# Three token blocks side by side in the second MLP product of the first batch, and weight pieces converted at other times

## The chip, the cores and the metric

The kernel runs on one core of a Trainium2 chip. The metric is the device time of one execution in microseconds (us); lower is better. A core has five engines that run their own instruction streams and wait for one another through semaphores: TensorE (PE: matrix products into the eight banks of PSUM, the accumulation memory), VectorE (DVE: elementwise work), ScalarE (ACT: activations and copies), GpSimd (POOL: elementwise work on SBUF, the on-chip memory) and SyncE (SP), which in this kernel issues every transfer from and to the main memory (HBM).

## The reference

For four batches of 768 tokens, eight heads of 40 features go through a gated recurrent cell; then a Fourier mixing and an MLP follow on rows of 320.

```python
# cell, for every time step
C = f_stab * C + i_stab * outer(v, k);  n = f_stab * n + i_stab * k
y = sigmoid(o_gate) * (C @ q) / max(|n . q|, 1)
# mixing and MLP, x = y with the heads side by side
mixed = real(fft(fft(x, axis=1), axis=2))
u = x + mixed
un = (u - mean(u)) / sqrt(var(u) + 1e-6)
out = u + relu(un @ w_ch1) @ w_ch2          # 320 -> 1280 -> 320
```

The two weight matrices reach the device as 64-bit floats, and the kernel turns them into 32-bit floats itself.

## The kernel before, in words

**The cell.** The recurrence is computed in chunks of 128 tokens (in two halves of 64 from the second batch on). For a chunk there are scores (`ps`), weights `W` that are loaded and passed through an exponential on ScalarE (L491), masked on GpSimd (L515) and multiplied with the scores on VectorE ("weighing", L672), the heads (`ph`), and the state `C`, to which VectorE adds each half's part (L667). The heads of a chunk are computed in two passes; between them ScalarE makes a copy of one element (L699) for which the second pass waits. VectorE finishes a chunk in five instructions (L712 to L720).

**The mixing.** VectorE folds the six blocks of 128 tokens in three steps (L812 to L824), TensorE multiplies by the sequence table (`pz`, `pzt`) and then by the feature table (`pu`), VectorE adds the result to x and takes mean and variance (L955 to L963), ScalarE centres the rows (`uc`, L971), TensorE transposes them (`put`, L978), and ScalarE copies that out (`uT`, L983).

**The MLP.** The six token blocks stand in two groups of three, in the order 0, 5, 1 and 4, 2, 3. For the first batch the first product (L1047, L1056) makes the hidden rows, one slot for each of ten blocks of 128 hidden units (f from 0 to 9) and each group; ScalarE applies the ReLU (L1071). The second product (`mlp_out`, L1181) accumulates over f in a bank `po`. It is cut into halves, f 0 to 4 and f 5 to 9, one slot each. When a block's product is complete, VectorE scales it and adds it to u (`residual`, L1187) and SP stores the block. The later batches use another scheme (L1118, L1237).

**The weights.** The 64-bit words are converted in ten pieces of 128x640: pieces 0 to 4 are the first weights, 5 to 9 the second, where piece 5 holds f 0 and 1, piece 6 f 2 and 3, and so on to piece 9 with f 8 and 9. A piece is loaded by SP into one of two buffers (`raw`, 640 KB), then *taken* by VectorE (L406, L408, which split exponent and mantissa bits into `e` and `m`, each with one buffer), *converted* by ScalarE (L413, L414) and *joined* by VectorE (L420, L422, L426). One piece must be joined before the next is taken. Pieces 3 and 4 are needed by the first product from the slots 35 and 36 on.

**What sets the order.** The program writes its order by hand. `at(slot, phase, fn)` enters a step in a plan, and `run` issues the plan sorted by slot and phase, so that each engine's instructions stand in that order. Within a slot the phases are EVAC 0, FILL 1, MAIN 2 and FILL_PE 3, with fractions between. The first batch's MLP begins in slot 31: slots 31 to 50 are the first product, slots 51 to 62 the second. The cell of the second batch runs beside it from slot 32, that of the third from slot 53, and the mixing of the second batch from slot 54. The list `when` gives slot and phase of each piece's take, convert and join; a piece after the fifth is loaded in the slot after the join of the piece two before. The pieces' own steps are in the class `Piece`:

```python
at(when[n - 2][2][0] + 1, FILL + 0.7, p.load)
for (s, phase), fn in zip(w, (p.take, p.convert, p.join)):
    at(s, FILL + phase, fn)
```

**The banks.** Four PSUM banks are handed out in the order of the string `turn`, a digit for each request of `bank`. From slot 28 on the scores and the heads of the cell have the other four.

**After the product.** `weight_sums` (L1096, four steps) forms sums of the first weights for the later batches, and `out_weight_sums` (L1209) sums of the second weights.

Of the kernel before, what the change touches and what calls it, by code (L numbers as in the profile page):

```python
# [19 lines left out]
L = 128  # L20
# [6 lines left out]
DM = H * D  # L27
DFF = 4 * DM
NFF = DFF // L
TAIL = DM - 2 * L  # L30
TG = NT // 2
# [22 lines left out]
def kernel(  # L54
# [14 lines left out]
    nc = tc.nc  # L69
# [13 lines left out]
    ps_early = ExitStack()  # L83
    ps_s, ps_h = (ps_early.enter_context(tc.tile_pool(name=n, bufs=2, space=PSUM)) for n in ("ps_s", "ps_h"))

    turn = iter("3210321032120312031230123012012301023130201320132013201320123021320321")

    def bank(name, shape, n=None):

        return ps_m.tile(shape, FP, name=name, tag=f"pm{next(turn) if n is None else n}")  # L90
# [16 lines left out]
    w2_sb = const.tile([L, NFF, DM], FP, name="w2_sb")  # L107
# [16 lines left out]
    def at(slot, phase, fn, *args):  # L124
        plan.setdefault((slot, phase), []).append((fn, args))
# [7 lines left out]
    EVAC, FILL, MAIN, FILL_PE = range(4)  # L133
# [248 lines left out]
    class Piece:  # L382
        def __init__(self, dst, src):
            self.dst, self.src, self.float = dst, src, src.dtype == FP
# [407 lines left out]

    class Mix:
        def __init__(self):
            self.pu, self.uc, self.pt, self.h = {}, {}, {}, {}

    mixes = {}

# [268 lines left out]
    def hidden(gr, f):  # L1067
        return hid[gr, f % 2][:, f // 2 * TG * L:(f // 2 + 1) * TG * L]
# [107 lines left out]
    def mlp_out(b, gr, i, half):  # L1176
        k = mixes[b]
        if half == 0:
            k.po = bank("po", [L, DM])
        for f in range(half * NFF // 2, (half + 1) * NFF // 2):  # L1180
            nc.tensor.matmul(k.po, hidden(gr, f)[:, i * L:(i + 1) * L], w2_sb[:, f, :], start=(f == 0), stop=(f == NFF - 1))  # L1181

    def residual(b, c, cols, po):

        k = mixes[b]
        u = k.u[:, c, cols]
        nc.vector.scalar_tensor_tensor(out=u, in0=po, scalar=k.rstd[:, c:c + 1], in1=u, op0=OP.mult, op1=OP.add)  # L1187

    def store(b, c):
        nc.sync.dma_start(out=out[b, c * L:(c + 1) * L, :], in_=xs[b][:, c, 0:DM])  # L1190

    def mlp_store(b, gr, i):
        c = ORDER[gr * TG + i]
        residual(b, c, slice(0, DM), mixes[b].po)
        store(b, c)


# [70 lines left out]
    def plan_mlp(b, s):  # L1268
        groups = range(NT // TG)
        for i in range(NFF // 2) if b > 0 else ():  # L1270
            for step in range(4):
                at(s, MAIN, mlp_block, b, i, step)
                s += 1
            end = i == NFF // 2 - 1
            for n, (gr, f) in enumerate(((1, 2 * i + 1), (1, 2 * i), (0, 2 * i))):
                at(*((s - 1, MAIN + (-0.1 if gr else 0.1)) if end else (s + n, MAIN + 0.5)), mlp_relu_in_place, gr, f)
        for gr in groups if b == 0 else ():
            for f in range(NFF):
                at(s, MAIN, mlp_in, b, gr, f)
                s += 1  # L1280
                if f % 2:
                    at(s, EVAC, mlp_relu, b, gr, f - 1)
                    at(s, EVAC, mlp_relu, b, gr, f)
        if b > 0:
            for j in range(1, 5):
                at(s - (5, 4, 3, 3)[j - 1], FILL_PE + 0.3, hidden_sums, 0, (j,), 0, NFF // 2 - 2)
            at(s, EVAC, hidden_sums, 0, (1, 2), NFF // 2 - 2, NFF // 2)
            at(s, MAIN + 0.1, hidden_sums, 0, (3, 4), NFF // 2 - 2, NFF // 2)
        for n in range(TG) if b > 0 else ():
            for step in range(4):  # L1290
                at(s, MAIN, mlp_out_pair, b, n, step)
                if n < TG - 1 and step > 1:
                    for j in (2 * step - 3, 2 * step - 2):
                        at(s, MAIN + 0.6, hidden_sums, n + 1, (j,))
                s += 1
        for gr in groups if b == 0 else ():
            for i in range(TG):
                for half in range(2):
                    at(s, MAIN, mlp_out, b, gr, i, half)
                    s += 1  # L1300
                at(s, EVAC, mlp_store, b, gr, i)

    ctx.enter_context(tc.manual_schedule())
    gates_pool = ExitStack()
# [3 lines left out]
    def plan_batch(b, s_mlstm, s_mix, s_mlp):  # L1308
        (plan_halves if b > 0 else plan_mlstm)(b, s_mlstm)
        done = [s_mlstm + n for n in ((16, 19, 22) if b == 0 else (18, 21, 22))]  # L1310
        assert s_mix >= done[-1] and s_mlp >= s_mix + 9
        late = [s_mlp + 2 * c for c in range(TG)]
        if b == 0:
            feat = [s_mix + 1, s_mix + 1, s_mlp + 3]
            turn = [s_mix + 2, s_mix + 3, s_mix + 4]
            add = turn + [s_mlp, s_mlp + 4, s_mlp + 5]
            late = [s_mlp + 2, s_mlp + 5, s_mlp + 7]
        else:
            feat = [s_mix + c for c in ((3, 4, 6) if b == 1 else (3, 4, 7))]
            add = [s_mix + c for c in ((4, 4, 5, 6, 7, 7) if b == 1 else (4, 5, 5, 6, 8, 9))]  # L1320
            turn = [s_mix + c for c in ((5, 6, 6) if b == 1 else (6, 7, 8))]
            late = [s_mix + c for c in ((7, 8, 8) if b == 1 else (9, 10, 10))]
            at(s_mlp, EVAC + 0.5, mlp_sums)
        plan_mix(b, s_mix, done, feat, add, turn + late)
        s = s_mlp + NFF + 2
        at(s, FILL + 0.6, mix_rstd, b)
        for n in range(3):
            at(s + 3 * n if b == 0 else s, FILL + 0.65, mix_rstd_step, b)
        plan_mlp(b, s_mlp)

    s_mlp = 31
# [2 lines left out]
    plan_batch(2, 53, 83, s_mlp + 2 * MLP_SLOTS)  # L1334
    plan_batch(3, 83, 115, s_mlp + 3 * MLP_SLOTS)
    for n in range(4):
        at(s_mlp + 2 * NFF + 1 + n, FILL + 0.4, weight_sums, n)
        at((56, 57, 58, 75)[n], FILL + 0.4, out_weight_sums, n)

    at(60, FILL + 0.4, lambda: nc.gpsimd.memset(ds_sb[0:1, 0, 0, :], 1.0))  # L1340

    when = [((2, 0.7), (4, 0.5), (6, 0.6)), ((6, 0.7), (7, 0.5), (8, 0.6)), ((11, 0.7), (13, 0.5), (22, 0.6))]
    when += [((22, 0.7), (23, 0.7), (27, 0.6)), ((27, 0.7), (28, 0.7), (32, 0.6))]
    when += [((33, 0.7), (34, 0.3), (34, 0.6)), ((34, 0.7), (35, 2.7), (36, 0.6))]
    when += [((s, 0.7), (s + 1, 0.7), (s + 2, 0.6)) for s in (36, 39, 42)]
    pieces = w1_pieces + w2_pieces
    for n, (w, p) in enumerate(zip(when, pieces)):
        if n > 4:
# [138 lines left out]
```

## Time and profile before

| | us |
|---|---|
| median of 3 runs | 402.24 (402.18 to 402.57) |
| the profiled execution | 402.53 |
| its span, first to last instruction | 400.8 |
| PE busy | 382.8 (96%) |
| DVE busy | 279.8 (70%) |
| ACT busy | 171.7 (43%) |
| POOL busy | 132.6 (33%) |
| L1181, the first batch's second product, 120 records | 34.2 busy, mean 0.435 |

Times are counted from the first instruction of the profiled execution. The profile shows two records of TensorE for each product that the program writes in 32-bit floats, so the 60 products of L1181 are 120 records. Matrix products overlap: a record lasts longer than the distance to the next. A line of the time-ordered view has the start, the duration, engine, line of the program, operation, output and inputs, the count, and in brackets the idle time of the engine before it and what released it. PEclk is the share of full speed at which TensorE's clock was granted.

### The profile page before, as it was taken

What the parts mean: (1) busy time and instruction counts of PE and PEld (TensorE: products, weight loads), DVE (VectorE), ACT (ScalarE), POOL (GpSimd) and SP (SyncE); (2) the same over time, 40 slices, a digit from 0 to 9 for tenths busy, and PEclk for the clock granted to TensorE, in tenths of its full rate; (3) what the DMA queues carried; (4) which work ended last, traced back from release to release, by engine and by line L of the source; (5) the groups of instructions that cost most, each with busy time, mean ns of one, the idle gap of its engine ahead of it and who ended that gap; (6) DMA issues with size and microseconds to landing.
All of it is one profiled execution on the core that took longest, in us unless ns stands there. A gap on an engine that the chain in (4) does not pass through costs nothing.

```text
span 400.8 us, 10588 instructions
## 1 busy us (share of the span) xinstructions
PE 382.8 (96%) x4174; PEld 278.4 (69%) x4174; DVE 279.8 (70%) x671; ACT 171.7 (43%) x481; POOL 132.6 (33%) x237
## 2 busy tenths in 40 slices
PE   8999899979999999998999989989999999999996
PEld 6877555545567677755569888845578986556996
DVE  7789988999665467485775598777764686336652
ACT  6987367655640232655462214544440023454000
POOL 5648513555863341253255124451310000020000
PEclk9999999979999999999999999999999999999999
DMA  7878499677286254447800526410000000000100
GB/s 222 288 228 246 151 241 275 191 191 220 72 190 169 60 155 127 118 133 185 186 1 28 138 71 194 145 38 2 0 0 18 17 34 33 2 0 0 34 33 34
DMA packets 25631, 44.78 MB, mean 112 GB/s; under 512 B 5727, under 2 KB 14766, under 8 KB 25454
## 3 DMA queue, kind: packets, MB, share of 16 engines
q1 hardware_dynamic: 25582, 44.11, 39.1%
q8 instruction: 33, 0.54, 0.6%
q14 instruction: 16, 0.13, 0.1%
HBM read 38.49 MB, written 4.12 MB: 106 GB/s over the span
## 4 chain that ended last, share of the span: by engine, by line
PE 67%; DVE 18%; DMA 6%; issue 4%; ACT 2%; POOL 1%; SPq 1%; DVEq 0%; POOLq 0%; ACTq 0%
PE po L1237 18%; PE pm L1118 14%; PE po L1181 8%; PE pm L1056 5%; PE ph L519 4%; PE pm L1123 4%; PE pu L935 3%; PE ps L519 2%; DMA Gb<-G_d 2%; DVE so L716 2%; DMA raw<-in_w 1%; PE pz L904 1%; PE pz L892 1%; DMA W<-M_d 1%; PE put L978 1%
## 5 line engine op out<-in xcount | busy, mean ns | idle before, releaser
L1187 DVE SCALAR_TENSOR_TENSOR x<-po,rstd,x 128x160 f32<-128x160 f32 (+1 forms) x69 | 27.0, 395 | 43.9 <-PE po L1237 36.8
L1127 DVE TENSOR_TENSOR h<-h,pm 128x384 f32<-128x384 f32 x60 | 30.5, 550 | 29.2 <-PE pm L1123 13.9
L652 POOL TENSOR_TENSOR C<-C,decB 128x164 f32<-128x164 f32 x30 | 16.0, 532 | 75.7 <-DVE C L667 64.7
L1118 PE MATMUL pm<-uT,w_sb 128*128 128x384 f32 x90 | 37.7, 506 | 2.1 <-DVE h L1127 1.3
L491 ACT ACTIVATE W<-W,colT 128x64 f32<-128x64 f32 x144 | 37.4, 339 | 0.0
L1181 PE MATMUL po<-w_sb,h 128*128 128x320 f32 x120 | 34.2, 435 | 0.0
L1056 PE MATMUL pm<-uT,w_sb 128*128 128x384 f32 x80 | 31.2, 528 | 0.3 <-DVE x L955 0.2
L515 POOL TENSOR_SCALAR_AFFINE_SELECT W<-W 64x512 f32<-64x512 f32 x36 | 27.2, 756 | 11.7 <-ACT W L491 10.4
L1002 POOL TENSOR_TENSOR t<-rstd 128x6 f32<-128x6 f32 x12 | 3.4, 281 | 81.9 <-DVE v L996 81.4
L1237 PE MATMUL po<-T,S 128*128 128x160 f32 x180 | 27.9, 302 | 1.5 <-DVE x L1187 1.5
L501 POOL TENSOR_TENSOR qg<-qk,Gb 128x512 f32<-128x512 f32 (+1 forms) x21 | 28.7, 1368 | 1.4 <-DMA kvt<-in_kv 0.8
L1181 PEld LDWEIGHTS po<-w_sb,h 128*128 128x128 f32 x120 | 22.3, 190 | 9.5 <-issue 0.6
L1237 PEld LDWEIGHTS po<-T,S 128*128 128x128 f32 x180 | 25.5, 190 | 3.2 <-DVE x L1187 2.0
L1118 PEld LDWEIGHTS pm<-uT,w_sb 128*128 128x128 f32 x90 | 15.5, 189 | 16.4 <-DVE h L1127 7.5
L1237 PE MATMUL po<-w_sb,h 128*128 128x160 f32 x180 | 26.3, 300 | 0.0
L1237 PEld LDWEIGHTS po<-w_sb,h 128*128 128x128 f32 x180 | 25.2, 190 | 1.4 <-DVE x L1187 0.3
L1174 ACT ACTIVATE h<-h 128x384 f32<-128x384 f32 x45 | 23.1, 520 | 2.0 <-DVE h L1127 2.0
L1123 PE MATMUL pm<-uT,w1t_sb 64*128 64x384 f32 x120 | 23.4, 508 | 0.0
L983 ACT COPY uT<-put 128x384 f32<-128x384 f32 x24 | 11.1, 476 | 27.5 <-PE put L978 27.5
L1056 PEld LDWEIGHTS pm<-uT,w_sb 128*128 128x128 f32 x80 | 15.0, 202 | 11.0 <-issue 3.2
L507 POOL TENSOR_TENSOR vw<-kvt,colT 128x328 f32<-128x328 f32 x23 | 18.0, 782 | 12.7 <-DVE colT L360 10.1
L971 ACT ACTIVATE uc<-x 128x384 f32<-128x384 f32 x24 | 14.4, 613 | 18.1 <-DVE x L963 12.1
(241 smaller groups left out, 843.3 us busy)
## 6 DMA issues: line engine op xcount, KB each, us to landing
kvt<-in_kv SPq DMA_DIRECT2D x24, 336.0 KB
qk<-in_qkT SPq DMA_DIRECT2D x48, 160.0 KB
raw<-in_w SPq DMA_DIRECT2D x10, 640.0 KB
Gb<-G_d SPq DMA_DIRECT2D x36, 128.0 KB
W<-M_d SPq DMA_DIRECT2D x36, 128.0 KB
so<-in_o SPq DMA_DIRECT2D x24, 160.0 KB
out<-x SPq DMA_DIRECT2D x24, 160.0 KB
x<-so SPq DMA_DIRECT2D x9, 140.0 KB
```

What stands on the lines that cost most here:

```text
L491: nc.scalar.activation(out=k.W[:, h, :], in_=M, func=AF.Exp, scale=-1.0, bias=colT[:, c, 0, b * H + h:b * H + h + 1])
L501: nc.gpsimd.tensor_tensor(out=k.qg[:, :, t], in0=k.qk[:, 0, :, t], in1=k.Gb[:, :, t], op=OP.mult)
L515: nc.gpsimd.affine_select(out=W, in_=W, compare_op=OP.is_ge, fill=0.0, base=base, pattern=[[0, H], [step, LH]], channel_multiplier=-1)
L519: nc.tensor.matmul(out, w, x, start=start, stop=True, skip_group_check=True)
L1056: nc.tensor.matmul(k.pm[i], w1_sb[:, ch, f0:f0 + L], u[2 * ch], start=(ch == 0 and not ahead), stop=(ch == 1 and ahead), skip_group_check= ...
L1118: nc.tensor.matmul(bank, w, u, start=start, stop=True, skip_group_check=True)
L1123: nc.tensor.matmul(bank, block(w1t_sb, i)[rows], mlp_u(gr, 1)[rows], start=False, stop=True, skip_group_check=True)
L1127: nc.vector.tensor_tensor(out=h, in0=h, in1=bank, op=OP.add)
L1174: nc.scalar.activation(out=h, in_=h, func=AF.Relu, scale=-1.0)
L1181: nc.tensor.matmul(k.po, hidden(gr, f)[:, i * L:(i + 1) * L], w2_sb[:, f, :], start=(f == 0), stop=(f == NFF - 1))
L1187: nc.vector.scalar_tensor_tensor(out=u, in0=po, scalar=k.rstd[:, c:c + 1], in1=u, op0=OP.mult, op1=OP.add)
L1237: nc.tensor.matmul(po, a[:, f], w[:, f], start=start and f == 0, stop=f == half - 1, skip_group_check=True)
```

## The change

The second product of the first batch's first group is put in another order. Before, each of the three token blocks is completed before the next is begun. Now the first halves (f 0 to 4) of all three blocks come first, each in its own bank, and then the second halves; each block's residual add and store follow its second half. The second group keeps its order. So that three blocks can be open at once, `k.po` becomes a dictionary by group and block, and one part of `turn` gives out the banks in another order (2031 for 2013).

The pieces are converted later. Piece 3 is joined in slot 31 where it was 27; piece 4 is taken in slot 31 (27) and joined in 33 (32); piece 5 is taken in slot 36 (33), 6 in 39 (34), 7 in 42 (36), 8 in 48 (39) and 9 in 51 (42, with its join now in slot 53). With the slots of the joins the loads of the pieces 5 to 9 move, from the slots 28, 33, 35, 37 and 39 to 32, 34, 39, 42 and 45. The four steps of `weight_sums` move two slots later.

```diff
-    turn = iter("3210321032120312031230123012012301023130201320132013201320123021320321")
+    turn = iter("3210321032120312031230123012012301023130201320132013203120123021320321")
...
         if half == 0:
-            k.po = bank("po", [L, DM])
+            k.po[gr, i] = bank("po", [L, DM])
         for f in range(half * NFF // 2, (half + 1) * NFF // 2):
-            nc.tensor.matmul(k.po, hidden(gr, f)[:, i * L:(i + 1) * L], w2_sb[:, f, :], start=(f == 0), stop=(f == NFF - 1))
+            nc.tensor.matmul(k.po[gr, i], hidden(gr, f)[:, i * L:(i + 1) * L], w2_sb[:, f, :], start=(f == 0), stop=(f == NFF - 1))
...
-        residual(b, c, slice(0, DM), mixes[b].po)
+        residual(b, c, slice(0, DM), mixes[b].po[gr, i])
         store(b, c)
...
         for gr in groups if b == 0 else ():
-            for i in range(TG):
-                for half in range(2):
-                    at(s, MAIN, mlp_out, b, gr, i, half)
-                    s += 1
-                at(s, EVAC, mlp_store, b, gr, i)
+            for n, (half, i) in enumerate(((0, 0), (0, 1), (0, 2), (1, 0), (1, 1), (1, 2)) if gr == 0 else
+                                          ((0, 0), (1, 0), (0, 1), (1, 1), (0, 2), (1, 2))):
+                at(s, MAIN, mlp_out, b, gr, i, half)
+                s += 1
+                if half == 1:
+                    at(s, EVAC, mlp_store, b, gr, i)
...
-        at(s_mlp + 2 * NFF + 1 + n, FILL + 0.4, weight_sums, n)
+        at(s_mlp + 2 * NFF + 3 + n, FILL + 0.4, weight_sums, n)
...
-    when += [((22, 0.7), (23, 0.7), (27, 0.6)), ((27, 0.7), (28, 0.7), (32, 0.6))]
-    when += [((33, 0.7), (34, 0.3), (34, 0.6)), ((34, 0.7), (35, 2.7), (36, 0.6))]
-    when += [((s, 0.7), (s + 1, 0.7), (s + 2, 0.6)) for s in (36, 39, 42)]
+    when += [((22, 0.7), (23, 0.7), (31, 0.5)), ((31, 0.7), (32, 0.7), (33, 0.6))]
+    when += [((s, 0.7), (s + 1, 0.7), (s + 2, 0.6)) for s in (36, 39, 42, 48, 51)]
```

More of the change, by code (lines that the diff above doesn't have):

```diff
@@ L794, in __init__ @@
         def __init__(self):
-            self.pu, self.uc, self.pt, self.h = {}, {}, {}, {}
+            self.pu, self.uc, self.pt, self.po = {}, {}, {}, {}
     mixes = {}
```

## The prediction

> **What bounds the kernel now.** I read the page first, then the instructions in time order on TensorE, then the same stretch on VectorE and ScalarE, then the stretches with their granted clock. The page says that TensorE is busy for 382.8 of 400.8 us, so time is won where TensorE stands or runs slowly. In its 40 slices (10.02 us each) one slice stands out:
>
> ```profile
> PE   8999899979999999998999989989999999999996
> PEclk9999999979999999999999999999999999999999
> ```
>
> The ninth slice, 80 to 90 us, has a 7 in both rows: TensorE waits and its clock is down. Stretches of 5 us (columns: sum, then busy us of PE, PEld, DVE, ACT, POOL, then clock, DMA share, GB/s) place it:
>
> ```profile
> 80.00:85.00 5.00, 3.14 (x117) 2.16 (x116) 4.67 (x9) 1.84 (x4) 1.16 (x2) 0.94 0.54 142
> 85.00:90.00 5.00, 3.87 (x27) 2.57 (x24) 4.43 (x7) 3.68 (x13) 4.59 (x5) 0.50 0.90 238
> ```
>
> VectorE is full (4.67 of 5). TensorE's instructions there (start, duration, in brackets the idle time before and its releaser):
>
> ```profile
> 81.53 0.42 PE L519 MATMUL ph<-kvt,W 64*64 64x41 f32 x16
> 83.82 0.69 PE L519 MATMUL ps<-qk 40*64 40x64 f32 x32 [1.86 <-DVE C L667]
> ...
> 86.17 0.66 PE L519 MATMUL ph<-kvt,W 64*64 64x41 f32 x16 [1.13 <-ACT warm L699]
> 86.76 0.90 PE L978 MATMUL put<-ident,uc 128*128 128x128 f32 x3
> 87.46 4.63 PE L1056 MATMUL pm<-uT,w_sb 128*128 128x384 f32 x8
> 92.02 0.92 PE L1047 MATMUL pm<-uT,w1t_sb 64*128 64x384 f32 x4
> ```
>
> Two waits, 1.86 and 1.13 us, and a group of eight matmuls at 4.63 us that takes 2.85 us at 99.20 us. Why VectorE's L667 was late, and ScalarE's L699:
>
> ```profile
> 80.19 0.81 DVE L420 SCALAR_TENSOR_TENSOR e<-raw,e 128x640 uint32<-128x640 uint32 x1
> 80.92 0.82 DVE L422 SCALAR_TENSOR_TENSOR m<-raw,m 128x640 f32<-128x640 uint32 x1
> 81.78 0.82 DVE L426 TENSOR_TENSOR w_sb<-m,e 128x640 f32<-128x640 f32 x1
> 82.64 0.49 DVE L406 TENSOR_SCALAR e<-raw 128x640 uint32<-128x640 uint32 x1
> 83.05 0.48 DVE L408 TENSOR_SCALAR m<-raw 128x640 uint32<-128x640 uint32 x1
> 83.45 0.32 DVE L667 TENSOR_TENSOR C<-C,ps 128x164 f32<-128x164 f32 x1
> ```
>
> ```profile
> 83.16 0.83 ACT L413 ACTIVATE e<-e,ebias 128x640 uint32<-128x640 uint32 x1 [3.64 <-DVE e L406]
> ...
> 84.52 1.05 ACT L491 ACTIVATE W<-W,colT 128x64 f32<-128x64 f32 x4
> 85.48 0.60 ACT L971 ACTIVATE uc<-x 128x384 f32<-128x384 f32 x1
> 85.98 0.13 ACT L699 COPY warm<-ph 1x1 f32<-1x1 f32 x1
> ```
>
> Three VectorE instructions finish one weight piece and two begin the next, all ahead of the state update L667 that TensorE needs; ScalarE stood 3.64 us for L406, and L699 stands behind that conversion. The chain of waits agrees: from 73 to 86 us it runs on VectorE, then ScalarE. From 87.5 to 170 us TensorE has no recorded idle time, so each us saved before that can reach the end.
>
> [...] The trace has one stretch at 0.5 after the start-up, 6.83 us from 84.4 us[...]. [...] L422 took 1.88 us at 84.91 with GpSimd at work, 0.82 us at 80.92 with GpSimd idle. I use this for ranges.
>
> **Part 1, pieces later (slots 27 to 44).** A piece costs VectorE 0.81 (L406 and L408, by starts 91.13 to 91.93) and 2.46 (L420, L422, L426, 80.19 to 82.64); ScalarE 0.74 and 0.65. Before, by slot 36 VectorE joins pieces 3 to 6 and takes piece 7. After, it has joined pieces 3 and 4 and taken piece 5. So about two pieces, 6.5 us, leave the crowded stretch. Walk through the new order with these durations:
> - VectorE, from 57.91: the mix add with its statistics (1.15, moved ahead of the join), join 3 (2.5 to 3.4 as before), take 4, then L665 when TensorE's ps is there (63.95), join 4 to about 67, the weighing, L667 to about 67.6. It then waits for pu (70.5 us), where it worked without a pause before.
> - ScalarE does the eight exponentials before conversion 4, then h and uc: uc comes about 0.8 us earlier and TensorE's 0.44 us wait at 66.52 goes. So does the 0.16 at 77.45. TensorE is 0.60 ahead by 81 us.
> - VectorE again: L667 after ps (74.2), fix-up and mix add (1.8), finish of a chunk (1.7), weighing (0.6), take 5 (0.8), L667 by about 79.7 to 80.5. TensorE wants it at 81.35. Wait gone: 1.87 (81.95 to 83.82).
> - ScalarE: conversion 5 from 79.1 to 80.5, exponentials to 81.6, uc to 82.1, L699 by 82.3; TensorE wants it at 82.5. The 1.13 goes, but with a slack of only 0.2.
> - With no such wait the clock should stay up. From 83.82 to 92.02 are 8.20 us, less 1.13 idle, 7.07; at full clock the same work is 1.16 (102.70 to 103.86) + 0.38 + 2.78 = 4.32. Gain 2.75.
>
> Sum: 0.60 + 1.87 + 1.13 + 2.75 = 6.35 us. SP's order moves too. The load for piece 5 (640 KB of raw) leaves when join 3 has freed its buffer, near 61.2 as before; that for piece 6 waits for join 4 (about 66) and holds the loads of the fourth chunk, which before left at 71.76 behind a like wait. Piece 7 is loaded where piece 9 was (88.16, less the lead), and nothing in place of the load at 81.77, behind which the row moves stood until 82.20; W of the fourth chunk still waits for TensorE's heads (75.22). Nothing is late there.
>
> Does the lead last to 117 us? I carried it slot by slot: at each of TensorE's next waits VectorE's L667 or weighing is 2 to 4 us early, and more later, since pieces 8 and 9 are gone from here.
>
> **Part 2, the second product.** Each half is 10 records, 2.69 us by spacing; the count stays 120, so the reordering costs TensorE nothing by itself. I use times of before; all shift by the lead. Slots 51 to 53 run from 117.65 to 125.93, then scores to 127.0, then slot 54. Before, the first block's second half ran in slot 52; now in slot 54, at 127.0, and its pairs of f 6, 7 need piece 8, those of f 8, 9 piece 9 at about 128.6. VectorE from 114.89: take 8 to 115.7, fold to 117.3, join 8 to 119.8 (up to 121.2 with GpSimd at work), chunk finish 1.65, take 9 to 122.3 (123.7), fold 1.6, join 9 to 126.4 without contention, up to 129.2 with (a join took 3.96 at 92.51). I take 127.5. So TensorE waits between 0 and 0.6, likely 0. Conversion 9 is ready at about 124, covered by the fold; it delays four exponentials from 120.1 to 125, and GpSimd's mask behind them to 126.5; their reader L672 came at 130.39. Conversion 8 puts L699 at 117.0 against a need at 117.28. VectorE's next work, L665, weight sum and the last fold, ends its first half at about 130 against the sequence product's 131.1; if the join came at 129.2, up to 0.9 more is lost. Without this cover, late joins count one for one.
>
> The residual adds move: the first from 123.43 to about 131, the second to 135, the third stays at 139.3. The bank of the second sequence product is the first block's: needed at 134.4, free at 131.5. The tail's is the second block's: 141.0 against 135. The weight sums move two slots, into VectorE's waits at 131 to 136 and 138 (2.4 us in all); the last pushes a chunk finish 0.8 us, ahead of the 2.26 idle at 147.21. Stores: the first no longer stands in SP before the loads at 124.40, so those go out sooner; the third holds the next loads to about 139.9 as before. Zero, cover named.
>
> I allow 0.3 us for the thin places (L699 twice, slot 54). Net 6.05. The profiled execution took 402.53 us (span 400.8, 1.7 around it), giving 396.5; the median is 402.24, giving 396.2.
>
> **Rivals.**
> - The early gain is only partial. Against it: the clock stretch starts right after the waits. For it: L699's slack of 0.2, and the cause of a clock fall is not shown by one event. Clock fall stays though the waits go: gain 3.6, 398.6. A wait of 1.5 stays and brings the fall: 396.2 + 4.25, about 400.4.
> - The new wait in slot 54. Join 9 comes 1.5 us or more after 128.6 and the clock falls as it did: 1.5 + 2.75, about 400.4. For it: every VectorE item ahead is in series (take, fold, finish, take, fold, join). Against: even with contention 129.2.
> - Slower than before: piece 9's load. It stands in SP behind the one-row move that before went out at 105.16, after GpSimd's row copies; take 9 wants the data by 121.5. If SP held it so long that join 9 were more than 3.6 us late (a landing after about 126), the wait plus 2.75 would eat the whole gain: at 5 us late 403.9. Against: that leaves 20 us for one load, and the load of piece 9 before, issued 88.16, was ready when taken at 99.86.
> - No effect: TensorE's early wait is replaced by an equal one at once, 402.2. VectorE's two pieces less speak against it.
>
> **Numbers.** Forecast 0.66, own range 395.4 to 397.2 (a little more gain if contention falls too; up to 1 us of thin waits). Partial gain 0.14, slot 54 with a clock fall 0.12, no effect 0.03, slower 0.05. Range 395.2 to 399.6: it takes in the forecast and the milder half of the partial cases. Faster by over 0.2% (0.8 us, about what a measurement tells from no change) 0.92, within 0.03, slower 0.05.
>
> **What would show it.** Right: no 0.5 clock after the start-up; ps of the second chunk pair starting near 81.3 and the four L1047 records near 85.7; the second product starting near 111.3; L1187 first about 8 us later relative to it; no DVE L426 among TensorE's releasers. Wrong: TensorE waiting over 1 us on L426 in slot 54, an L699 wait over 0.5, or a clock stretch anywhere, each with its price above.

## The result, and the profile after

The changed kernel takes 396.27 us (median of 4 runs, 395.51 to 396.52) against 402.21 us for the kernel before (402.01 to 402.57): ratio 0.9843, interval 0.9824 to 0.9862. The prediction said 396.2 us.

The profiled execution took 395.51 us, its span is 393.8 us. It was 0.68 us ahead before the change could act: VectorE's L362, its last instruction ahead of the moved join of piece 3, starts at 57.01 us (before 57.69), and the MLP's first group of eight L1056 at 58.50 us (before 59.18). A second profile of the same kernel (below, first experiment) has that group at 59.50 us, so this is scatter of the start. I therefore give distances from this group. They agree in the two profiles of the changed kernel to 0.01 us up to the second product:

| from the first L1056 group to | before | after | after, second profile |
|---|---|---|---|
| the L1047 group behind the former waits | 32.84 | 26.36 | 26.37 |
| the first L1181 | 58.47 | 52.18 | 52.18 |
| the end of the span | 341.62 | 335.30 | 335.40 |

So 6.48 us were won between 59 and 92 us, 0.19 given back by the second product, and the rest of the kernel kept the lead of 6.3 us.

The page of the changed kernel, TensorE's busy tenths and its clock in 40 slices:

```profile
PE   8999899999999999998999989989999899999996
PEclk9999999999999999999999999999999999999999
```

The ninth slice, a 7 in both rows before, is a 9 in both. Stretches of 5 us of the changed kernel (length, busy us of PE, of PEld, which are TensorE's weight loads, of DVE, ACT and POOL, then clock, DMA share, GB/s):

```profile
80.00:85.00 5.00, 4.50 (x102) 3.00 (x96) 4.76 (x9) 3.94 (x14) 4.85 (x5) 1.00 0.67 191
85.00:90.00 5.00, 5.00 (x139) 3.30 (x140) 4.71 (x8) 3.56 (x10) 3.09 (x4) 1.00 0.96 285
```

TensorE stands 0.50 us in ten, and the clock is full. VectorE is no less full than before (4.76 and 4.71 of 5, where it was 4.67 and 4.43): what changed is what it does first. TensorE's instructions there, in time order (start, duration, group, idle time and releaser):

```profile
79.93 0.68 PE L519 MATMUL ps<-qk 40*64 40x64 f32 x32
80.43 0.51 PE L519 MATMUL ps<-vw,kvt 64*40 64x41 f32 x32
81.43 0.44 PE L519 MATMUL ph<-kvt,W 64*64 64x41 f32 x16 [0.50 <-ACT warm L699]
81.80 0.55 PE L978 MATMUL put<-ident,uc 128*128 128x128 f32 x3
82.19 2.75 PE L1056 MATMUL pm<-uT,w_sb 128*128 128x384 f32 x8
84.86 0.92 PE L1047 MATMUL pm<-uT,w1t_sb 64*128 64x384 f32 x4
```

The scores (`ps`) no longer wait for L667, one wait of 0.50 us for L699 is left of the 1.13, and the eight L1056 take 2.75 us in place of 4.63. VectorE in the same view of the changed kernel:

```profile
77.90 0.48 DVE L406 TENSOR_SCALAR e<-raw 128x640 uint32<-128x640 uint32 x1
78.30 0.48 DVE L408 TENSOR_SCALAR m<-raw 128x640 uint32<-128x640 uint32 x1
78.71 0.32 DVE L667 TENSOR_TENSOR C<-C,ps 128x164 f32<-128x164 f32 x1
79.28 0.96 DVE L420 SCALAR_TENSOR_TENSOR e<-raw,e 128x640 uint32<-128x640 uint32 x1 [0.26 <-ACT e L413]
80.17 1.89 DVE L422 SCALAR_TENSOR_TENSOR m<-raw,m 128x640 f32<-128x640 uint32 x1
82.09 1.15 DVE L426 TENSOR_TENSOR w_sb<-m,e 128x640 f32<-128x640 f32 x1
```

Only a take stands ahead of L667 now, and the join comes behind it. ScalarE of the changed kernel:

```profile
78.42 0.83 ACT L413 ACTIVATE e<-e,ebias 128x640 uint32<-128x640 uint32 x1 [0.34 <-DVE e L406]
79.16 0.72 ACT L414 ACTIVATE m<-m 128x640 f32<-128x640 uint32 x1
79.78 1.05 ACT L491 ACTIVATE W<-W,colT 128x64 f32<-128x64 f32 x4
80.74 0.60 ACT L971 ACTIVATE uc<-x 128x384 f32<-128x384 f32 x1
81.24 0.13 ACT L699 COPY warm<-ph 1x1 f32<-1x1 f32 x1
```

It waits 0.34 us for the take (3.64 before), but a conversion of 1.4 us still stands ahead of L699. Last, the second product of the changed kernel on TensorE, and the end of join 9 on VectorE:

```profile
110.68 8.34 PE L1181 MATMUL po<-w_sb,h 128*128 128x320 f32 x30
120.03 2.96 PE L1181 MATMUL po<-w_sb,h 128*128 128x320 f32 x10
```

```profile
118.44 1.27 DVE L422 SCALAR_TENSOR_TENSOR m<-raw,m 128x640 f32<-128x640 uint32 x1
119.74 1.15 DVE L426 TENSOR_TENSOR w_sb<-m,e 128x640 f32<-128x640 f32 x1
```

The ten records of slot 54 run without a wait. By their spacing of 0.27 us, two records to a product, f 8 is wanted at about 121.6 us, and the join ends at 120.9: 0.7 us to spare.

### The profile page after: what moved, and what is told of

Read it like the earlier page. It is cut to its first block, busy times and chain, and to the rows that moved or that the text cites. A ratio compares the mean times of both kernels' runs of the same rounds, so it can differ in the third digit from the quotient of the medians.

```text
span 393.8 us, 10580 instructions
## 1 busy us (share of the span) xinstructions
PE 378.9 (96%) x4174; PEld 276.4 (70%) x4174; DVE 277.9 (71%) x671; ACT 172.1 (44%) x481; POOL 134.3 (34%) x237
## 4 chain that ended last, share of the span: by engine, by line
PE 74%; DVE 18%; issue 3%; ACT 3%; POOL 1%; DVEq 0%; ACTq 0%; POOLq 0%
PE po L1237 18%; PE pm L1118 15%; PE po L1181 8%; PE pm L1056 6%; PE ph L519 4%; PE pm L1123 4%; PE pu L935 3%; PE ps L519 3%; PE pm L1047 2%; PE put L978 2%; DVE h L1127 2%; PE pz L904 1%; PE pz L892 1%; DVE so L716 1%; DVE x L1187 1%
## 5 line engine op out<-in xcount | busy, mean ns | idle before, releaser
L1187 DVE SCALAR_TENSOR_TENSOR x<-po,rstd,x 128x160 f32<-128x160 f32 (+1 forms) x69 | 26.9, 394 | 41.5 <-PE po L1237 36.8
L1118 PE MATMUL pm<-uT,w_sb 128*128 128x384 f32 x90 | 37.7, 506 | 2.0 <-DVE h L1127 1.3
L491 ACT ACTIVATE W<-W,colT 128x64 f32<-128x64 f32 x144 | 37.5, 338 | 1.1 <-DMA W<-M_d 1.1
L1181 PE MATMUL po<-w_sb,h 128*128 128x320 f32 x120 | 34.3, 435 | 0.0
L1056 PE MATMUL pm<-uT,w_sb 128*128 128x384 f32 x80 | 29.2, 500 | 0.1
L1181 PEld LDWEIGHTS po<-w_sb,h 128*128 128x128 f32 x120 | 22.3, 190 | 9.5 <-issue 0.6
L501 POOL TENSOR_TENSOR qg<-qk,Gb 128x512 f32<-128x512 f32 (+1 forms) x21 | 27.4, 1306 | 1.9 <-DMA qk<-in_qkT 1.3
L1118 PEld LDWEIGHTS pm<-uT,w_sb 128*128 128x128 f32 x90 | 15.5, 189 | 16.3 <-DVE h L1127 7.4
L507 POOL TENSOR_TENSOR vw<-kvt,colT 128x328 f32<-128x328 f32 x23 | 19.3, 838 | 12.2 <-DMA qk<-in_qkT 10.1
L1056 PEld LDWEIGHTS pm<-uT,w_sb 128*128 128x128 f32 x80 | 14.1, 189 | 9.6 <-issue 1.9
```

Source lines behind the costliest of these rows:

```text
L491: nc.scalar.activation(out=k.W[:, h, :], in_=M, func=AF.Exp, scale=-1.0, bias=colT[:, c, 0, b * H + h:b * H + h + 1])
L501: nc.gpsimd.tensor_tensor(out=k.qg[:, :, t], in0=k.qk[:, 0, :, t], in1=k.Gb[:, :, t], op=OP.mult)
L1056: nc.tensor.matmul(k.pm[i], w1_sb[:, ch, f0:f0 + L], u[2 * ch], start=(ch == 0 and not ahead), stop=(ch == 1 and ahead), skip_group_check= ...
L1118: nc.tensor.matmul(bank, w, u, start=start, stop=True, skip_group_check=True)
L1181: nc.tensor.matmul(k.po[gr, i], hidden(gr, f)[:, i * L:(i + 1) * L], w2_sb[:, f, :], start=(f == 0), stop=(f == NFF - 1))
```

## The experiments

Each time stands beside runs of the kernel before on the same chip. Where a kernel is said to be so much later or sooner, its distance from the first L1056 group is compared with that of the changed kernel, unless the kernel before is named.

**The changed kernel again**, the same program, as the measure for the others.

> The changed kernel once more, as the measure for the runs beside it. Ratio to before 0.984, as measured (about 396.3 us).

Measured 396.21 us against 402.93, ratio 0.984 (0.9827 to 0.9853). It repeats the result and gives the second profile of the table above.

**1. The new order alone.** The changed kernel with the pieces' slots of the kernel before.

```diff
-    when += [((22, 0.7), (23, 0.7), (31, 0.5)), ((31, 0.7), (32, 0.7), (33, 0.6))]
-    when += [((s, 0.7), (s + 1, 0.7), (s + 2, 0.6)) for s in (36, 39, 42, 48, 51)]
+    when += [((22, 0.7), (23, 0.7), (27, 0.6)), ((27, 0.7), (28, 0.7), (32, 0.6))]
+    when += [((33, 0.7), (34, 0.3), (34, 0.6)), ((34, 0.7), (35, 2.7), (36, 0.6))]
+    when += [((s, 0.7), (s + 1, 0.7), (s + 2, 0.6)) for s in (36, 39, 42)]
```

> The reordered second product, its banks and the later weight sums, with the pieces converted where they were before. Theory A (the whole gain comes from the pieces that left VectorE between 57 and 86 us): no change, 402.2 us within 0.6, both waits at 82 and 85 us and the half clock still there, TensorE without a wait in the second product. Rival B (the reordering frees something of its own): 399.5 us or less.

Measured 402.73 us against 402.74, ratio 0.9993 (0.9978 to 1.0009). Both early waits (1.86 us for L667, 0.68 us for L699) and the half clock, 6.83 us long, are there. Three blocks side by side cost nothing and win nothing by themselves, to within the 1 us that the interval leaves open.

**2. The pieces alone, product in its old order.** The kernel before, with pieces 3 to 7 at the new slots; since the old order wants all pieces one slot after the product's start, 8 and 9 are taken in slots 45 and 48 rather than 48 and 51.

```diff
-    when += [((22, 0.7), (23, 0.7), (27, 0.6)), ((27, 0.7), (28, 0.7), (32, 0.6))]
-    when += [((33, 0.7), (34, 0.3), (34, 0.6)), ((34, 0.7), (35, 2.7), (36, 0.6))]
-    when += [((s, 0.7), (s + 1, 0.7), (s + 2, 0.6)) for s in (36, 39, 42)]
+    when += [((22, 0.7), (23, 0.7), (31, 0.5)), ((31, 0.7), (32, 0.7), (33, 0.6))]
+    when += [((s, 0.7), (s + 1, 0.7), (s + 2, 0.6)) for s in (36, 39, 42, 45, 48)]
```

> Pieces 3 to 7 as in the change, pieces 8 and 9 taken in the slots 45 and 48 so that they are joined before the second product begins, which keeps its old order. Theory A (VectorE has room in the slots 45 to 50, where it idled 1.7 and 2.1 us, so the reordering is not needed for the gain): 396.3 us within 0.8, no half clock. Rival C (the last two pieces need the cover that the reordered product gives): 398.5 us or more, with a TensorE wait between slot 45 and slot 52.

Measured 399.67 us, ratio 0.9933 (0.991 to 0.9955): about half of the gain. Up to the L1047 group its profile equals the changed kernel (26.36); the second product starts 2.55 us later. TensorE and ScalarE of this kernel in time order:

```profile
107.80 0.44 PE L519 MATMUL ph<-kvt,W 64*64 64x41 f32 x16 [1.74 <-ACT warm L699]
```

```profile
104.56 0.83 ACT L413 ACTIVATE e<-e,ebias 128x640 uint32<-128x640 uint32 x1 [4.99 <-DVE e L406]
105.30 0.72 ACT L414 ACTIVATE m<-m 128x640 f32<-128x640 uint32 x1
105.92 0.85 ACT L1071 ACTIVATE h<-pm 128x384 f32<-128x384 f32 x2
106.66 1.05 ACT L491 ACTIVATE W<-W,colT 128x64 f32<-128x64 f32 x4
107.62 0.13 ACT L699 COPY warm<-ph 1x1 f32<-1x1 f32 x1
```

Conversion 8, which waited 4.99 us for its take, holds the ReLU, the exponentials and L699 behind it. It is the old wait for L699 once more, at another place. The profiled execution has no half clock (mean clock 1.000); the four others have a mean clock of 0.995 or 0.996, which is what one stretch of 3.41 us makes of it (0.996 in experiment 6 with three copies). So the profile shows the loss without the clock, and the median with it.

**3. Can that be mended without the new order?** Two kernels, on the one above. In the first, conversion 8 goes behind an L699.

```diff
+    when[8] = ((45, 0.7), (47, 2.7), (48, 0.6))
```

> The kernel before with the pieces later, but the second product in its old order (as in e2_pieces_alone), and conversion 8 put behind L699 on ScalarE. Theory A (half of the gain was lost in e2_pieces_alone because conversion 8, which waits for VectorE's take, stood ahead of the exponentials and L699, and the order of the second product matters only through where pieces 8 and 9 can be put): the 1.74 us wait for L699 before the second product goes, 396.5 to 398 us. Rival (pieces 8 and 9 crowd VectorE there whatever ScalarE does, so the other order of the product is what wins): 399.5 us as in e2_pieces_alone, with the wait at a weighing, a L667 or the join instead.

Measured 399.97 us, ratio 0.9936 (0.9924 to 0.9949). The test does not separate ScalarE's order from the product's: the wait at 107 us is gone, but the later join 8 stands in the same slot as take 9, so conversion 9 now starts at 111.99 ahead of the next L699, and TensorE waits 2.25 us there, with a stretch of 3.41 us at half clock. The second moves piece 9 one slot on and behind an L699 too.

```diff
+    when[8] = ((45, 0.7), (47, 2.7), (48, 0.6))
+    when[9] = ((49, 0.7), (50, 2.7), (51, 0.6))
```

> The kernel before with the pieces later and the second product in its old order, both conversions 8 and 9 behind an L699 (9 is taken in slot 49, converted in 50 behind L699, joined in 51). Theory A (the new order of the product is needed: in the old one f 8 and 9 are wanted one slot after the product's start, at about 115.6 us, and a join that begins at 113.9 us and takes 3 to 4 us comes at 117 to 118 us): no wait for L699 before the product, but one of 1.5 to 2.5 us for L426 within it, and with it perhaps the half clock: 398 to 400 us. Rival (the gain in e2_pieces_alone was lost only to ScalarE's order): no wait in the product, 396.3 to 397.3 us.

Measured 402.61 us, ratio 0.9991 (0.9977 to 1.0006). TensorE and VectorE of this kernel in time order:

```profile
120.09 5.59 PE L1181 MATMUL po<-w_sb,h 128*128 128x320 f32 x14 [3.44 <-DVE w_sb L426]
```

```profile
115.06 1.64 DVE L716 SCALAR_TENSOR_TENSOR so<-so,den 128x320 f32<-128x320 f32 x1
...
119.21 0.82 DVE L426 TENSOR_TENSOR w_sb<-m,e 128x640 f32<-128x640 f32 x1
```

ScalarE's order is right here: the second product starts only 0.36 us later than in the changed kernel. But join 9 ends at 120.0 us, TensorE waits 3.44 us for it within the product, and 3.41 us of half clock follow. The wait is longer than the 1.5 to 2.5 us expected; 1.15 us of it go to L716 ahead of the join, which takes 0.49 us in most places and 1.64 us here with GpSimd at work. The join ends 8.0 us after the product's start; in the changed kernel it ends 10.2 us after it and is in time, since two more half products stand ahead of its reader. So the new order is what makes the late pieces free: in the old one the profiles of the three placements tried end 2.7 to 5.9 us later (by the ratios about 4 to 6 us). Other placements were not tried.

**4. The slack of the new order.** The changed kernel with join 9 one slot later.

```diff
+    when[9] = ((51, 0.7), (52, 0.7), (54, 0.6))
```

> The changed kernel with the join of piece 9 one slot later, behind the state copy, a weight sum and the last fold on VectorE. Theory A (the cover in slot 54 is about 0.8 us, and beyond it every us of a late join is a wait of TensorE): join 9 ends 4 to 5.5 us later, TensorE waits 3.5 to 4.8 us for L426, and the clock falls: 396.3 + 4.2 + 2.75 = 403.2 us, 400.5 us if the clock stays. Rival E (the join has slack of several us, TensorE is not held): 396.3 us.

Measured 402.8 us, ratio 1.0007 (0.9995 to 1.002): the whole gain is gone. TensorE of this kernel in time order, and its clock in a stretch of 5 us:

```profile
126.20 2.50 PE L1181 MATMUL po<-w_sb,h 128*128 128x320 f32 x4 [3.97 <-DVE w_sb L426]
```

```profile
125.00:130.00 5.00, 3.80 (x9) 3.00 (x10) 2.97 (x6) 0.00 (x0) 0.40 (x1) 0.50 0.00 0
```

One slot costs 6.9 us at the end. Of these 3.97 us are waiting, and 2.6 us are by my estimate the clock: it is at 0.50 for 6.83 us, of which TensorE works 5.2, and I count half of that as lost against the full clock.

**5. Which wait brings the half clock?** The kernel before with conversion 7 behind L699 and its join one slot later, which takes away the second early wait and leaves the first.

```diff
+    when[7] = ((36, 0.7), (38, 2.7), (39, 0.6))
```

> The kernel before with one line more: conversion 7 goes behind L699 in slot 38, its join into slot 39. Of the two waits of TensorE at 82 to 86 us only the second (1.13 us, L699) is taken away; the first (1.86 us, L667 behind the join and the take) stays. If one wait of 1.86 us is enough for the half clock, the gain is the 1.1 us of the wait alone: 401.1 us, a ratio of 0.997. If both waits together make the clock fall, it stays up and the gain is 1.1 + 2.75 = 3.9 us: 398.4 us, a ratio of 0.990.

Measured 400.7 us, ratio 0.9953 (0.994 to 0.9966): between the two. TensorE in time order:

```profile
84.39 0.69 PE L519 MATMUL ps<-qk 40*64 40x64 f32 x32 [1.86 <-DVE C L667]
...
86.54 3.75 PE L1056 MATMUL pm<-uT,w_sb 128*128 128x384 f32 x8
```

In this execution a half clock follows the single wait of 1.86 us, but it lasts 3.41 us (85.15 to 88.56) where it lasted 6.83. In the kernel before, the second wait, of 1.13 us, stood within that stretch; without it the stretch is half as long. By the L1047 group the kernel is 2.02 us ahead of the kernel before: 1.13 of wait and about 0.9 of clock.

**6. The wait put back into the changed kernel.** Copies on ScalarE ahead of L699 in slot 38, into a buffer that nothing reads: eight as shown, and three in a second kernel.

```diff
+    def hold(n):
+        for i in range(n):
+            nc.scalar.copy(out=s_last[:, 0:2 * L], in_=rest)
+
+    at(38, FILL_PE + 0.45, hold, 8)
```

> The changed kernel with three more copies of 128x256 on ScalarE ahead of L699 in slot 38. The wait grows from 0.5 to about 1.4 us. Theory A (a wait well under 1.8 us costs its own length alone, as the 1.74 us in e2_pieces_alone): 396.3 + 0.9 = 397.2 us, no stretch at half clock. Rival (any wait over 1 us brings the half clock): 398.9 us.

> The changed kernel with eight more copies of 128x256 on ScalarE ahead of L699 in slot 38[...]; their output is read by nothing. TensorE's wait for L699 at 81 us grows from 0.5 to about 2.8 us. Theory A (one wait of 1.9 us or more brings half the clock for 3.4 us, as with the single wait in e10_second_wait_gone): 396.3 + 2.3 + 1.7 = 400.3 us. Rival (the clock needs both waits of the kernel before): 398.6 us. Rival (the wait is caught up by a later slack): 396.3 us.

Measured 398.64 us, ratio 0.9885 (0.9867 to 0.9903), with three, and 401.33 us, ratio 0.9959 (0.9944 to 0.9974), with eight. A copy took 0.42 us (three took 1.26, eight 3.44), so the waits are longer than the 1.4 and 2.8 us that I had estimated. TensorE with three:

```profile
83.27 0.44 PE L519 MATMUL ph<-kvt,W 64*64 64x41 f32 x16 [1.68 <-ACT warm L699]
...
84.05 4.41 PE L1056 MATMUL pm<-uT,w_sb 128*128 128x384 f32 x8
88.39 0.92 PE L1047 MATMUL pm<-uT,w1t_sb 64*128 64x384 f32 x4
```

and with eight:

```profile
85.42 0.67 PE L519 MATMUL ph<-kvt,W 64*64 64x41 f32 x16 [3.86 <-ACT warm L699]
...
86.71 4.34 PE L1056 MATMUL pm<-uT,w_sb 128*128 128x384 f32 x8
```

Theory A was wrong for three copies: the wait of 1.68 us is followed by a half clock of 3.41 us. At the L1047 group this kernel is 2.87 us later: 1.18 of wait and 1.69 of clock, which is half of 3.41. With eight it is 5.50 us later: 3.36 of wait and 2.14 of clock (6.83 us at half, of which TensorE stood 2.34). So a wait in this place costs its own length and, where the clock falls, 1.7 to 2.1 us more; the prediction's 2.75 us for the clock is of that kind, and in experiment 4 the clock cost 2.6.

**7. The waits filled with work.** The kernel before with six extra products into unused columns of the heads' bank, four for the first wait and two for the second. They are written into the bank in which the heads of that chunk are summed, and the output of this kernel is wrong.

```diff
+    def fill_wait(n):
+        for i in range(n):
+            nc.tensor.matmul(banks["heads"][:, 0, 2 * L:], rest[:, 0:L], rest, start=True, stop=True, skip_group_check=True)
+
+    at(38, FILL_PE + 1, fill_wait, 4)
+    at(38, FILL_PE + 2.9, fill_wait, 2)
```

> The kernel before with six more products of zeros of 256 columns on TensorE, four in its first wait (82.0 us) and two in its second (85.0 us), into columns of a bank that nothing reads. The waits stay as long as they were, only TensorE is busy in them. Theory A (the half clock follows from the idle time, and costs 2.75 us by itself): no half clock, 402.2 - 2.75 = 399.5 us within 0.8. Rival D (the half clock comes for another reason, or the slow products were hidden behind VectorE's lateness, so that the clock costs nothing by itself): 402.0 us or more.

Measured 406.53 us, ratio 1.0097 (1.0071 to 1.0124). TensorE in time order:

```profile
86.66 3.42 PE L1362 MATMUL ph<-rest 128*128 128x256 f32 x8 [4.22 <-ACT warm L699]
```

The filling products write into the bank that L699 reads, so they themselves waited for it, 4.22 us, and the clock fell all the same, to 0.50 for 3.41 us from 87.06 us on. The test says nothing on its question; the two kernels above answer it.

**8. The last 0.5 us.** The changed kernel with conversion 5 behind L699 (the first line alone); then with conversion 6 too (both lines).

```diff
+    when[5] = ((36, 0.7), (38, 2.7), (39, 0.6))
+    when[6] = ((39, 0.7), (41, 2.7), (42, 0.6))
```

> The changed kernel with one line more: piece 5 is converted in slot 38, behind L699 on ScalarE, and joined in slot 39. Theory A (the remaining 0.5 us wait of TensorE for L699 at 81.4 us comes from the conversion that stands ahead of it, and TensorE has no other slack there): the wait goes, about 395.8 us, 0.5 us under the changed kernel. Rival (something else is next, L667 or uc, within the same microsecond): no difference, 396.3 us. Rival (the later join 5 pushes an L667 past TensorE's need): 397 us or more.

> The changed kernel with conversions 5 and 6 both behind an L699 (slots 38 and 41) and their joins in slots 39 and 42. In e6_convert5_late the wait at 81 us went, and one of 0.93 us for L699 at 90 us came, behind conversion 6. Theory A: both waits go and nothing comes in their place, about 395.8 us (0.998 of the changed kernel's ratio). Rival (the delay passes on to piece 7 and the weighing behind it): 396.3 us or more.

Measured 396.94 us, ratio 0.9863 (0.9849 to 0.9878), and 397.45 us, ratio 0.9862 (0.9836 to 0.9887): neither is better than the changed kernel (0.984). TensorE and ScalarE of the first:

```profile
90.38 0.44 PE L519 MATMUL ph<-kvt,W 64*64 64x41 f32 x16 [0.93 <-ACT warm L699]
```

```profile
87.14 0.83 ACT L413 ACTIVATE e<-e,ebias 128x640 uint32<-128x640 uint32 x1 [2.36 <-DVE e L406]
```

The wait at 81 us is gone and the L1047 group comes 0.71 us sooner. But join 5, one slot later, pushes take 6, conversion 6 stands waiting ahead of the next L699, and 0.93 us are lost there; the second product starts 0.30 us later than in the changed kernel. With conversion 6 moved as well, the wait appears at 98.06 us (0.84 us for L699, 0.21 for an L667 ahead of it). The delay is handed from piece to piece.

## Why the prediction was right, and where it was not

**Waits ahead of 81 us, and 1.87 for L667.** Predicted 0.60 and 1.87. At the last heads' products ahead of the wait (81.53 before, 79.70 after) TensorE is 1.15 us ahead by distance: uc comes sooner (0.61, where the record had 0.44 idle), the wait for L955 is gone (0.33, where it had 0.16), the rest is smaller. From these products to the scores it was 2.29 us and is 0.23, so the wait was worth 2.06. Causes and signs are as predicted; the idle times in the record were too small as a price, since the ends of products are modelled there, and distances between starts are the better measure.

**The wait for L699.** Predicted to go (1.13) with a slack of 0.2. That step failed: 0.50 remained, just at the limit that the prediction had named as a sign of being wrong, and 0.63 was won. In times of before, L699 was done at 82.05, as predicted (by 82.3), but TensorE came to it at 81.6 and not at 82.5: the larger lead of the first point moved the need, and the slack of 0.2 became a wait.

**The clock.** Predicted 2.75. What is left of the measured gain for it is 6.48 − 1.15 − 2.06 − 0.63 = 2.64, where the 0.63 is still a difference of idle times. The runs with the wait put back show it as an effect of the wait: 1.69 with 3.41 us of half clock, 2.14 with 6.83.

**Sum.** Predicted 6.35, measured 6.48 at the L1047 group. The errors of the steps, +0.55, +0.19, −0.50 and −0.11, nearly cancel. The causes were right; that their sum came within 0.13 us is luck.

**What carries on to 117 us.** I had allowed 0.3 for thin places, and 0.19 was given back. Of the loads up to slot 44 I wrote that nothing is late, and neither TensorE, VectorE nor ScalarE waited for one there. Behind that, at 112.42 us, ScalarE's L491 stood 1.14 us for a load of W, which I had not seen; TensorE did not wait for it.

**The second product.** Join 9 was predicted for 127.5 in times of before; it ended at 120.89, which with the lead of 6.97 at that place is 127.9, inside the range of 126.4 to 129.2. The lengths of the joins came as drawn: L422 took 1.83 us in join 8 and 1.27 in join 9, both with GpSimd at work, and 0.82 with GpSimd idle in the trace of before (at 80.92 us). No wait of TensorE came, as predicted. That the reordering costs nothing was shown alone (experiment 1). The first L1187 comes 13.98 us after the product's start, before 5.78: 8.2 later, predicted about 8.

**The rivals.** The rival of a new wait in slot 54 was priced at 1.5 + 2.75; when a later join was forced it cost 3.97 + 2.6 (experiment 4), so the cause that it named and its price for the clock are right, and the margin by which it did not come is 0.7 us. The rival of a partial gain with a remaining wait of 1.5 us was put at 400.4; a wait of 1.68 us gave 398.64, because there the clock was down for 3.41 us, not for 6.83. The late load of piece 9 did not come: take 9 ran at 115.31, without a wait.

## What to carry to other kernels

An instruction that works ahead for later (a weight piece, a conversion) belongs behind those that the bottleneck engine waits for in the same stretch; what it costs is not its own time but the queue behind it, and here also TensorE's clock (2.64 us by the remainder above). Moving it back is only free as long as its own reader is late enough, and reordering the reader's independent work, at no cost on its engine, can buy that room; measure what margin is left (here 0.7 us, and one slot more took back the whole gain). A wait that is moved out of one slot should be looked for in the next one behind the same helper.

## What the runs showed of the hardware

**Idle time ahead of the half clock.** Between the start and the last microseconds of the kernels profiled here the half clock lasted 3.41 or 6.83 us. I took the idle time over the 3.41 us ahead of each fall, the length of the shorter stretch: TensorE stood 1.52 us (eight copies), 1.68 (three copies), 1.86 (before, and experiments 1 and 5), 2.25 and more in the others. In experiment 7 it had stood 1.21 us in the 3.41 us before those, and the clock was still at 1.00. The least idle time ahead of a fall is thus 1.52 of 3.41 us here.

**How long it lasted.** The stretch lasted 6.83 us where TensorE stood again in its first 3.41 us: 0.68 us (experiment 1), 1.13 (before), 1.58 (experiment 4), 2.34 (eight copies). It lasted 3.41 us where TensorE stood 0.25 us (the second kernel of experiment 3) or not at all (three copies, and experiments 5 and 7).

**One case without a fall.** No half clock follows the wait of 1.74 us of experiment 2 in the profiled execution (mean clock 1.000), though one follows 1.68 with three copies. Here are 3.41 us of experiment 2 that hold this wait (106.06 to 107.80 us) but for 0.03 us, and below them the 3.41 us ahead of the fall with three copies (columns as for the stretches of 5 us):

```profile
106.09:109.50 3.41, 1.70 (x20) 1.19 (x21) 3.34 (x6) 2.78 (x10) 3.41 (x3) 1.00 0.64 174
80.58:83.99 3.41, 1.73 (x99) 1.56 (x92) 3.38 (x4) 2.95 (x10) 3.35 (x3) 1.00 0.63 168
```

TensorE is about equally busy in both (1.70 and 1.73 us), so its idle time alone does not tell the two apart. The work differs: with three copies 1.46 of the 1.73 us are the small products of L519 (40 or 64 rows), in experiment 2 only 0.44 of the 1.70 are, and the rest is L1056 with 128 rows. The 3.41 us with 1.52 us idle ahead of a fall (eight copies) were also nearly all L519 (1.72 of 1.89 us). Whether the size of the products matters was not shown.

**The fall is not the same in every execution.** The mean clock of a profiled execution is 0.996 with 3.41 us of half clock (three copies) and 0.991 with 6.83 us (before). Of the six executions of experiment 5 two have 1.000, of the 22 of the second kernel of experiment 3 three have 0.999 (400.3 to 401.0 us, where the median is 402.6), and of the six with both conversions moved in experiment 8 two have 0.996 (398.9 and 399.0 us, the others at most 397.5). One profile of a kernel with such a wait does not tell what its other executions do. The changed kernel has 0.999 or 1.000 in all eight of its executions.
